# Windowed attention with block summaries, a causal gate and two projections: the order of every engine written by hand

## The chip, the cores and the metric

The kernel runs on one core of a Trainium2 chip. The core has five engines with a queue each, which the profile names PE (TensorE, matrix products; PEld is its loading of the stationary operand), DVE (VectorE), ACT (ScalarE), POOL (GpSimd) and SP (here only the issuer of DMAs). Every engine works off its own queue in order. An instruction whose inputs are not there yet waits, and all that stands behind it on that engine waits too. The metric is device time in microseconds (us); the executions measured took 295.82 us in the median of three (294.51 to 297.52).

## The reference, cut to what matters

```
B, H, S, D = 4, 8, 768, 64;  block, window = 32, 16
k_sum = max over each block of 32 keys;  v_sum = mean over each block of 32 values
scores_l = q k^T / sqrt(D)          # kept where |i - j| < 16, else -1e9
scores_s = q k_sum^T / sqrt(D) + log(32)
a = softmax([scores_l, scores_s]);  y = a @ [v, v_sum]
x = y as (B, S, 512)
gate = sigmoid(sum over 5 taps of conv_w[t] * x shifted by 4 - t rows, causal)
out = (gate * (x @ w_val)) @ w_out
```

All arrays are float32 as the reference sees them; the weights reach the kernel as 8-byte numbers, which it takes apart itself.

## The kernel before, in words

**Tiles.** A batch of 768 rows is cut into three groups of 256 rows (`SG`), so there are 12 groups, g = 0 to 11. Of a group's four pairs of heads, two make a *unit*: 24 units, u = 0 to 23, two to a group. A unit goes through these stages; the names are those that the changed code gives them, the lines those of the kernel before.

- Scores: 16 float32 matmuls (L314) into one PSUM tile `s`, of which there is only one buffer. DVE scales, masks and takes the row's minimum with one custom instruction per tile, eight a unit (`sn`, `nm`, L327; *snorm* in the change). ACT takes the exponentials, eight a unit, with the row sums as a by-product (L338, *exps*).
- Norm: DVE adds 1e-9 and takes the reciprocal (`ri`, L347, L348), POOL multiplies the probabilities by it, two instructions of 480 columns (L351).
- Transposes: four on PE into one PSUM tile `pt` with a single buffer (L364, *tp*), and a copy of it by ACT into `pts` (L365, *pcopy*), twice a unit.
- x: attention times values, 16 matmuls (L381; group 0 has 16 more, L383) into one PSUM tile `x`. ACT copies it out (*xout*): rounded as `xh` (L391) and whole as `xf` (L392), and POOL takes the difference `xl` (L394).
- Gate: for groups 0 to 4 ACT writes the last tap into PSUM tile `g` (L404, *ginit*); in later groups DVE does (L408). DVE adds the four other taps, eight instructions a unit (L412, *taps*). They read `xf` and four halo columns before it, which POOL fills when a group begins (L291, L293). ACT takes tanh (L416, *gate*).

Per group come the projections. *val* (L446, `proj_val`) is two tiles, each of 24 matmuls that build a float32 product from the halves `xh`, `xl` and the two halves of `wv`; group 0 uses plain float32 (L431). A val tile is evicted by DVE, which multiplies it by the gate (`gf`, L450), by ACT, which rounds (`gh`, L451), and by POOL, which takes the rest (`gl`, L452). *out* (L464, `proj_out`) is two tiles of 12 matmuls each over `gh`, `gl` and the halves of `wo`; ACT evicts it (`ob`, L470) and SP stores it. PSUM holds three tiles `pp` for projections.

**Side work.** For each later batch, four pieces of keys are reduced by DVE (`prep_k`, L123, L133), four pieces of values by a tree of additions on POOL (`prep_v`, L144). PE transposes the four sums (`prep_vs`, L179), ACT copies them, and DMAs spread them into the value tile (`fill_vs`, L191). The weights are converted to float32 at the start by ACT and DVE (`to_f32`, L204 to L211) and split into halves by ACT and POOL (`split_w`, L246, L247).

**What sets the order.** A loop over steps s (L541) emits, for each step, side work, the norm of unit s - 1, projections, x and gate of unit s - 2, scores of unit s, projections, and the transposes of unit s - 1. Of this text only SP keeps the order, and in the first two steps PE within a step; the others are ordered by the framework's scheduler, from its own estimate of times. Projections are issued from a budget (`PROJ_RATE`, `VAL_COST`, `OUT_COST`, L483). Side work has due steps in tables (L46 to L50).

Of the kernel before, what the change touches and what calls it, by code (L numbers as in the profile page):

```python
# [41 lines left out]
LAG_N, LAG_T, LAG_AV = 1, 1, 2  # L42
PROJ_RATE = 2.03
VAL_COST, OUT_COST = 2.64, 2.6
ACT_TAP_G = 5
LOADS = "k0 q0 m k1 q1 n0 i k2 q2 n1 k3 q3 n2 n3 v0 c w0 w1 w2 w3 Q"  # L46
CONVERT = {"wv": (0, 0, 1, 0), "wo": (3, 4, 3, 5)}
SPLIT = {"wv": (6, 2, 5, 2), "wo": (6, 5, 6, 6)}
LOAD_K = ((2, 3, 4, 4), (0, 1, 2, 3))
PREP_K = ((3, 4, 5, 5), (2, 2, 4, 4))  # L50
# [3 lines left out]
def tile_attention_then_gated_conv(  # L54
# [145 lines left out]
    def to_f32(dst, raw, n, nm, bufs):  # L200
# [3 lines left out]
        nc.scalar.activation(sc, high.bitcast(F32), AF.Copy, scale=REBIAS)  # L204
        hi = sc.bitcast(U32)
# [5 lines left out]
        nc.vector.scalar_tensor_tensor(d, hi, 0x80000000, d, ALU.bitwise_and, ALU.bitwise_or)  # L211
# [37 lines left out]
    def load_cw():  # L249
        dst = cwt.rearrange("p a k -> p (a k)")  # L250
        if not wide:
            nc.sync.dma_start(dst, cw)
# [3 lines left out]
        to_f32(dst, raw, NPR * NK, "cw", 1)  # L256

    def load_w4(nm, src, ks):
        for k in ks:
            load_w(nm, src, k, wk, ("gh", "gl")[k % 2])  # L260
# [5 lines left out]
        w=lambda i: load_w4("wv", wv, (i,)),  # L266
# [31 lines left out]
    def stage_s(u):  # L298
        b, th, hp = units[u]
        g = b * NTH + th  # L300
        sp = ps_s.tile([P, 2, 512], F32, tag="s", name=f"s_{u}")
        sn = wk.tile([P, NP, KW], F32, tag="sn", name=f"sn_{u}")
        p = wk.tile([P, NP, KW], F32, tag="p", name=f"p_{u}", bufs=3)
        nm = wk.tile([P, NP], F32, tag="nm", name=f"nm_{u}", bufs=4)
        rs = wk.tile([P, NP], F32, tag="rs", name=f"rs_{u}", bufs=4)
        for r in range(2):
            pr = 2 * hp + r
            for j in range(TPU // 2):
                for e in range(2):
                    for h in range(2):  # L310
                        i = 2 * j + e
                        t = th * TPU + i
                        c = 2 * r + j
                        nc.tensor.matmul(  # L314
                            sp[64 * e : 64 * e + 64, h, c * KW : c * KW + KW],
                            qbd[g % NQB][64 * h : 64 * h + 64, pr, i * QT : i * QT + QT],
                            ktile[b, pr][64 * h : 64 * h + 64, STEP * t : STEP * t + KW],
                            start=True,
                            stop=True,
                        )  # L320
            for j in range(TPU // 2):
                for h in range(2):
                    t = th * TPU + 2 * j
                    mv = 0 if t == 0 else (2 if t == NT - 2 else 1)
                    n = TPU * r + 2 * j + h
                    c = 2 * r + j
                    nc.vector.tensor_tensor_reduce(  # L327
                        sn[:, n, :],
                        sp[:, h, c * KW : c * KW + KW],
                        mask[:, mv, :],  # L330
                        -1.0 / math.sqrt(D),
                        3.0e38,
                        ALU.add,
                        ALU.min,
                        nm[:, n : n + 1],
                    )
        for n in range(NP):
            nc.scalar.activation(  # L338
                p[:, n, :], sn[:, n, :], AF.Exp, bias=nm[:, n : n + 1], scale=-1.0,
                accum_out=rs[:, n : n + 1],  # L340
            )
# [16 lines left out]
    def stage_t(u, r):  # L358
# [3 lines left out]
        pt = ps_t.tile([P, TPU, P], F32, tag="pt", name=f"pt_{u}_{r}")  # L362
        for i in range(TPU):
            nc.tensor.transpose(pt[:KW, i, :], s["p"][:, TPU * r + i, :], ident)  # L364
        nc.scalar.copy(s["pts"][:, TPU * r : TPU * r + TPU], pt[:KW])  # L365

    def stage_av(u):
        b, th, hp = units[u]
        g = b * NTH + th
        s = st.pop(u)  # L370
        xp = ps_x.tile([P, 2, SG], F32, tag="x", name=f"x_{u}")
        v = vtile[g]
        for r in range(2):
            for i in range(TPU):
                for h in range(2):
# [16 lines left out]
        nc.scalar.copy(x[:, prs, c0 : c0 + SG], xp)  # L392
# [239 lines left out]
```

## Time and profile before

| | |
|---|---|
| executions | 295.82 us median, 294.51 to 297.52 |
| the profiled execution | 294.14 us |
| its span, first to last instruction | 292.4 us |
| mean granted clock of TensorE | 0.977 |
| instructions | 7376 |
| HBM read, written | 34.51 MB, 6.29 MB |

Times in the profile are in microseconds from the start of the span; the mean of one instruction is in ns. In a row of the timeline the first number is the start, the second the duration of the merged instructions, `x4` their count, and the bracket holds the idle time of the engine before them with what ended it. In a group's row (`L412 DVE ...`) the busy time and the mean follow the bar, then the idle time before the group and its releasers. In a table by stretches the columns are the length and then, for PE, PEld, DVE, ACT and POOL, busy time and count, then the granted clock, the DMA share and GB/s. A float32 matmul leaves two records on PE. Pieces of the chain of waits give start, length, engine and line.

### The profile page before, as it was taken

What the parts mean: (1) busy time and instruction counts of PE and PEld (TensorE: products, weight loads), DVE (VectorE), ACT (ScalarE), POOL (GpSimd) and SP (SyncE); (2) the same over time, 40 slices, a digit from 0 to 9 for tenths busy, and PEclk for the clock granted to TensorE, in tenths of its full rate; (3) what the DMA queues carried; (4) which work ended last, traced back from release to release, by engine and by line L of the source; (5) the groups of instructions that cost most, each with busy time, mean ns of one, the idle gap of its engine ahead of it and who ended that gap; (6) DMA issues with size and microseconds to landing.
All of it is one profiled execution on the core that took longest, in us unless ns stands there. A gap on an engine that the chain in (4) does not pass through costs nothing.

```text
span 292.4 us, 7376 instructions
## 1 busy us (share of the span) xinstructions
PE 248.7 (85%) x2660; PEld 201.0 (69%) x2660; DVE 209.9 (72%) x761; ACT 183.1 (63%) x593; POOL 150.2 (51%) x187
## 2 busy tenths in 40 slices
PE   1238475999998999979978889799999998999995
PEld 0126363777886777957856767597887887898893
DVE  1949799597866887782769879987976697963710
ACT  1429472686883968877387648696678667745131
POOL 1132847468675397295059566646454355270421
PEclk9999959599999999999999999999999999999999
DMA  7999940771367854701828908426054340101011
GB/s 220 402 261 313 327 182 17 214 288 56 110 152 246 234 187 121 239 8 36 231 101 194 319 18 207 189 92 154 2 151 129 103 127 23 72 2 72 2 72 72
DMA packets 15148, 43.44 MB, mean 149 GB/s; under 512 B 2512, under 2 KB 3280, under 8 KB 13936
## 3 DMA queue, kind: packets, MB, share of 16 engines
q1 hardware_dynamic: 15111, 42.98, 47.9%
q8 instruction: 21, 0.34, 0.5%
q14 instruction: 16, 0.12, 0.1%
HBM read 34.51 MB, written 6.29 MB: 140 GB/s over the span
## 4 chain that ended last, share of the span: by engine, by line
PE 40%; DMA 23%; DVE 18%; ACT 8%; POOL 4%; SPq 4%; issue 3%; ACTq 0%; POOLq 0%; DVEq 0%
PE val L446 14%; PE out L464 13%; DMA k<-in_kT_dram 8%; DMA v<-in_vw_dram 7%; DVE g L412 7%; PE x L381 4%; DMA out_dram<-ob 4%; ACT p L338 4%; PE s L314 4%; PE pt L364 3%; DMA raw_wo<-in_wo_dram 2%; DVE sn L327 2%; SPq L191 2%; DMA vT<-in_vT_dram 2%; DVE ks L123 2%
## 5 line engine op out<-in xcount | busy, mean ns | idle before, releaser
L412 DVE SCALAR_TENSOR_TENSOR g<-xf,cwt,g 128x256 f32<-128x256 f32 x192 | 93.5, 487 | 9.0 <-ACT g L404 4.7
L338 ACT ACTIVATE p<-sn,nm 128x120 f32<-128x120 f32 x192 | 73.9, 392 | 22.3 <-DVE nm L327 22.1
L446 PE MATMUL val<-xh,wv 128*128 128x256 f32 x352 | 69.0, 285 | 0.6 <-ACT ob L470 0.6
L351 POOL TENSOR_TENSOR p<-p,ri 128x480 f32<-128x480 f32 x48 | 47.4, 1007 | 29.4 <-DVE ri L348 19.8
L464 PE MATMUL out<-wo,gh 128*128 128x512 f32 x192 | 59.3, 400 | 0.5 <-DVE gf L450 0.5
L446 PEld LDWEIGHTS val<-xh,wv 128*128 128x128 f32 x352 | 55.3, 188 | 3.2 <-issue 1.1
L327 DVE CUSTOM_DVE_ANT_0 sn<-s,mask 128x120 f32<-128x120 f32 x192 | 43.4, 277 | 14.2 <-PE s L314 14.1
L446 PE MATMUL val<-xl,wv 128*128 128x256 f32 x176 | 50.6, 288 | 0.7 <-POOL xl L394 0.7
L314 PE MATMUL s<-k,qbd 64*64 64x120 f32 x768 | 37.8, 292 | 12.4 <-DVE nm L327 6.9
L394 POOL TENSOR_TENSOR xl<-xf,xh 128x512 fp32r<-128x512 f32 x22 | 28.4, 1291 | 27.6 <-ACT xf L392 27.6
L452 POOL TENSOR_TENSOR gl<-gf,gh 128x512 fp32r<-128x512 f32 x24 | 31.2, 1301 | 20.6 <-ACT gh L451 20.6
L144 POOL TENSOR_TENSOR vT<-vT 128x384 f32<-128x384 f32 (+3 forms) x48 | 27.7, 582 | 23.6 <-DMA vT<-in_vT_dram 15.9
L464 PEld LDWEIGHTS out<-wo,gh 128*128 128x128 f32 x192 | 34.6, 188 | 7.4 <-issue 0.8
L381 PE MATMUL x<-pts,v 120*64 120x64 f32 x768 | 35.7, 231 | 4.6 <-ACT pts L365 3.9
L464 PE MATMUL out<-wo,gl 128*128 128x512 f32 x96 | 36.7, 407 | 2.4 <-POOL gl L452 2.4
L381 PEld LDWEIGHTS x<-pts,v 120*64 120x64 f32 x768 | 28.7, 139 | 14.5 <-issue 5.3
L314 PEld LDWEIGHTS s<-k,qbd 64*64 64x64 f32 x768 | 23.1, 140 | 22.6 <-DVE nm L327 6.5
L364 PE MATMUL pt<-ident,p 128*120 128x128 f32 x192 | 32.2, 291 | 6.3 <-ACT pts L365 3.2
L338 ACT ACTIVATION_READ_ACCUMULATOR p<-sn,nm 128x1 f32 x192 | 37.5, 195 | 0.0
L365 ACT COPY pts<-pt 120x512 f32<-120x512 f32 x48 | 28.1, 586 | 10.9 <-PE pt L364 10.9
L446 PEld LDWEIGHTS val<-xl,wv 128*128 128x128 f32 x176 | 33.0, 188 | 2.8 <-issue 1.3
L364 PEld LDWEIGHTS pt<-ident,p 128*120 128x120 f32 x192 | 22.2, 143 | 12.5 <-POOL p L351 4.8
(52 smaller groups left out, 277.2 us busy)
## 6 DMA issues: line engine op xcount, KB each, us to landing
k<-in_kT_dram SPq DMA_DIRECT2D x16, 478.0 KB
vT<-in_vT_dram SPq DMA_DIRECT2D x16, 384.0 KB
out_dram<-ob SPq DMA_DIRECT2D x24, 256.0 KB
qbd<-in_qT_dram SPq DMA_DIRECT2D x11, 512.0 KB
v<-in_vw_dram SPq DMA_DIRECT2D x11, 512.0 KB
v<-in_vw_dram SPq DMA_DIRECT2D x22, 128.0 KB
raw_wv<-in_wv_dram SPq DMA_DIRECT2D x4, 512.0 KB
raw_wo<-in_wo_dram SPq DMA_DIRECT2D x4, 512.0 KB
```

The source lines that it names most:

```text
L314: nc.tensor.matmul(sp[64 * e : 64 * e + 64, h, c * KW : c * KW + KW], qbd[g % NQB][64 * h : 64 * h + 64, pr, i * QT : i * QT + QT], ktile[ ...
L327: nc.vector.tensor_tensor_reduce(sn[:, n, :], sp[:, h, c * KW : c * KW + KW], mask[:, mv, :], -1.0 / math.sqrt(D), 3.0e38, ALU.add, ALU.mi ...
L338: nc.scalar.activation(p[:, n, :], sn[:, n, :], AF.Exp, bias=nm[:, n : n + 1], scale=-1.0, accum_out=rs[:, n : n + 1],)
L351: nc.gpsimd.tensor_tensor(s["p"][:, w], s["p"][:, w], ri[:, w].unsqueeze(2).broadcast_to([P, TPU, KW]), ALU.mult,)
L364: nc.tensor.transpose(pt[:KW, i, :], s["p"][:, TPU * r + i, :], ident)
L365: nc.scalar.copy(s["pts"][:, TPU * r : TPU * r + TPU], pt[:KW])
L381: nc.tensor.matmul(dst, v[:, i, c0 : c0 + D], src, start=True, stop=g > 0)
L394: nc.gpsimd.tensor_tensor(G["xl"][:, prs, :], x[:, prs, c0 : c0 + SG], G["xh"][:, prs, :].bitcast(F32), ALU.subtract,)
L412: nc.vector.scalar_tensor_tensor(gt[:, r], x[:, pr, o : o + SG], cwt[:, pr, o : o + 1], gt[:, r], ALU.mult, ALU.add,)
L446: nc.tensor.matmul(pp[:, r], w[:, ci, cs], G[x][:, ci, :], start=(n == 0), stop=(n == 11))
L452: nc.gpsimd.tensor_tensor(G["gl"][:, cos, :], gf, G["gh"][:, cos, :].bitcast(F32), ALU.subtract)
L464: nc.tensor.matmul(pp, G[gx][:, ci, si * P : si * P + P], w[:, ci, :], start=(n == 0), stop=(n == 11))
```

## The change

The scheduler's freedom is taken away: one region around the whole kernel keeps the order of the program text on all engines. The text is rewritten for this. The stages are cut into single functions (the body of each is as before, except where named below), and a `step` emits them. The first four units and the conversions are laid out op by op ahead of step 4.

```diff
-LOADS = "k0 q0 m k1 q1 n0 i k2 q2 n1 k3 q3 n2 n3 v0 c w0 w1 w2 w3 Q"
-CONVERT, SPLIT, PROJ_RATE, VAL_COST, OUT_COST, LAG_*
+LOADS = "k0 q0 m k1 q1 n0 i k2 q2 n1 k3 q3 n2 n3 v0 c Q w0 w1 w2 w3 v1 o0 o1 o2 o3"
+LOAD_K = (-4, -3, -2, -1)
+PREP_K = (-2, -1, -1, 0)
+PREP_V = (-3, -2, -1, 0)
...
-        nc.scalar.activation(sc, high.bitcast(F32), AF.Copy, scale=REBIAS)
+        nc.scalar.activation(sc, high.bitcast(F32), AF.Prelu, scale=REBIAS, alpha=-(2.0**32))
-        nc.vector.tensor_scalar(d, hi, 3, None, ALU.logical_shift_left)
+        nc.vector.tensor_scalar(d, low, 29, None, ALU.logical_shift_right)
         nc.vector.scalar_tensor_tensor(
-            d, low, 29, d, ALU.logical_shift_right, ALU.bitwise_or
+            d, sc.bitcast(U32), 3, d, ALU.logical_shift_left, ALU.bitwise_or
         )
-        nc.vector.scalar_tensor_tensor(d, hi, 0x80000000, d, ALU.bitwise_and, ALU.bitwise_or)
...
+    def proj():
+        if not queue:
+            return lambda: None
+        mm, ev, g, i = queue.pop(0)
+        pp = mm(g, i)
+        return lambda: ev(g, i, pp)
...
+    def late_loads(s):
...
+                if w == PREP_K[i]:
+                    prep_k(b, i)
+                if w == PREP_V[i]:
+                    prep_v(b, i)
+            if w == 0:
+                prep_vs(b)
+                fill_vs(b * NTH)
...
+    def step(s, late=lambda: None):
+        early_loads(s)
+        norm(s - 1)
+        ev = proj()
+        mm_x(s - 2)
+        ev()
+        xout(s - 2)
+        ginit(s - 2)
+        mm_s(s, 0)
+        mm_s(s, 1)
+        snorm(s, 0)
+        snorm(s, 1)
+        tp(s - 1, 0)
+        exps(s, 0)
+        pcopy(s - 1, 0)
+        exps(s, 1)
+        taps(s - 2)
+        ev = proj()
+        tp(s - 1, 1)
+        pcopy(s - 1, 1)
+        ev()
+        gate(s - 2)
+        if units[s - 2][2] == NHP - 1 and s > 3:
+            queue_proj((s - 2) // NHP)
+        late()
+        late_loads(s)
...
+    prep_k(0, 0)
+    mm_s(0, 0)
+    snorm(0, 0)
+    exps(0, 0)
...
+    exps(2, 0)
+    split_w("wv", 1)
+    conv_w("wv", 3)
+    exps(2, 1)
+    early_loads(2)
+    mm_s(3, 0)
+    mm_s(3, 1)
+    ppv = [val_mm(0, 0)]
+    taps(0)
+    gate(0)
+    ginit(1)
+    norm(2)
+    snorm(3, 0)
+    snorm(3, 1)
...
+    val_ev(0, 1, ppv[1])
+    split_w("wv", 3)
+    conv_w("wo", 0)
+    split_w("wo", 0)
+    late_loads(3)
+
+    def late4():
+        for k in range(1, 4):
+            conv_w("wo", k)
+            split_w("wo", k)
+        queue.extend((out_mm, out_ev, 0, si) for si in range(SG // P))
+
+    step(4, late4)
+    for s in range(5, NU + 2):
+        step(s)
+    while queue:
+        proj()()
...
-    ... tc.manual_schedule(engines={_mybir.EngineType.SP}):
+    ... tc.manual_schedule():
```

(The guards `if s < NU` and the like, which leave out stages at both ends, are cut from `step`.) Further:

- The queue of projections holds both val tiles, then both out tiles of a group. Each `proj()` takes one item from its head, emits its matmuls and gives back a function that emits its eviction; between the two stand x, or the second half of the transposes.
- Within a val tile the eight matmuls per row half that read `xh` come first and the four that read `xl` last; within an out tile the eight that read `gh` first, the four that read `gl` last. Group 0's val uses one PSUM tile for both row halves and one eviction for both.
- The key and value pieces of batch b are loaded in steps 6b - 4 to 6b - 1 and prepared in steps 6b - 3 to 6b, at the end of a step. `wo` and the second value tile are loaded with the first loads, `wo` in the buffers of `xh` and `xl`; the first loads of q for group 1 stand ahead of `wv`.
- The conversion of the convolution's weights is taken out of their load and stands after unit 1's norm.

More of the change, by code (lines that the diff above doesn't have):

```diff
@@ L249, in load_cw @@
     def load_cw():
[L250 removed]
         if not wide:
[L252 removed]
+            nc.sync.dma_start(cwt.rearrange("p a k -> p (a k)"), cw)
             return
@@ L296, in group, with mm_s @@
         return grp[g]
-    def stage_s(u):
+    def mm_s(u, r):
         b, th, hp = units[u]
         g = b * NTH + th
[L301 to L321, printed above, removed]
@@ L474, in tile_attention_then_gated_conv @@
     queue = []
-    issued = set()
-    def can_issue(item):
-        f, g, i = item
-        if f is proj_val:
-            return len(ready["wv" if g else "wvf"]) == 4
-        return (g, NHP - 1) in issued and len(ready["wo"]) == 4
-    def run_proj(budget):
-        while budget > 0:
-            item = next((it for it in queue if can_issue(it)), None)
-            if item is None:
-                break
-            queue.remove(item)
-            f, g, i = item
-            f(g, i)
-            if f is proj_val:
-                issued.add((g, i))
-            budget -= VAL_COST if f is proj_val else OUT_COST
-        return min(budget, PROJ_RATE)
@@ new lines, in late_loads @@
+    def late_loads(s):
+        g, hp = divmod(s, NHP)
+        for b in range(1, B):
+            w = s - b * NTH * NHP
+            for i in range(NPR):
+                if w == PREP_K[i]:
[5 more added lines that the diff above has]
+                fill_vs(b * NTH)
+        if hp == NHP - 1 and 1 <= g < NG - 1:
+            load_v(g + 1)
+            if (g + 1) % NTH:
+                fill_vs(g + 1)
@@ new lines, in tile_attention_then_gated_conv @@
+    prep_k(0, 0)
+    mm_s(0, 0)
+    snorm(0, 0)
+    exps(0, 0)
+    prep_k(0, 1)
+    mm_s(0, 1)
+    prep_v0(0)
+    snorm(0, 1)
+    exps(0, 1)
+    prep_k(0, 2)
+    mm_s(1, 0)
+    prep_v0(1)
+    snorm(1, 0)
+    norm(0)
+    exps(1, 0)
+    prep_k(0, 3)
+    tp(0, 0)
+    mm_s(1, 1)
+    pcopy(0, 0)
+    prep_v0(2)
+    snorm(1, 1)
+    tp(0, 1)
+    prep_v0(3)
+    exps(1, 1)
+    pcopy(0, 1)
+    place_vs0()
+    fill_vs(1)
+    norm(1)
+    conv_cw()
+    tp(1, 0)
+    pcopy(1, 0)
+    mm_x(0)
@@ new lines, in tile_attention_then_gated_conv @@
+    tp(1, 1)
+    pcopy(1, 1)
+    xout(0)
+    ginit(0)
+    conv_w("wv", 0)
+    mm_s(2, 0)
+    mm_s(2, 1)
+    snorm(2, 0)
+    snorm(2, 1)
+    mm_x(1)
+    xout(1)
+    conv_w("wv", 1)
+    split_w("wv", 0)
+    conv_w("wv", 2)
+    exps(2, 0)
[12 more added lines that the diff above has]
+    snorm(3, 1)
+    exps(3, 0)
+    tp(2, 0)
@@ new lines, in tile_attention_then_gated_conv @@
+    pcopy(2, 0)
+    val_ev(0, 0, ppv[0])
+    exps(3, 1)
+    split_w("wv", 2)
+    ppv.append(val_mm(0, 1))
+    taps(1)
+    gate(1)
+    tp(2, 1)
+    pcopy(2, 1)
+    early_loads(3)
+    norm(3)
+    val_ev(0, 1, ppv[1])
[9 more added lines that the diff above has]
+    step(4, late4)
```

287 lines of the change are left out of this document (139 added, 148 removed).

## The prediction, made before the changed kernel was run

> **What bounds the kernel now.** I read the page's busy shares and its clock row first, then the pace of the units (the reciprocal of the softmax sums, one per unit, is a good clock), then single stretches of the timeline.
>
> ```profile
> PE 248.7 (85%) x2660; PEld 201.0 (69%) x2660; DVE 209.9 (72%) x761; ACT 183.1 (63%) x593; POOL 150.2 (51%) x187
> ...
> PEclk9999959599999999999999999999999999999999
> ```
>
> ```profile
> 71.12 0.20 DVE L348 RECIPROCAL ri<-ri 128x8 f32<-128x8 f32 x1
> 256.39 0.20 DVE L348 RECIPROCAL ri<-ri 128x8 f32<-128x8 f32 x1
> ```
>
> ```profile
> 172.40:191.70 19.30, 16.26 (x192) 12.46 (x191) 18.44 (x75) 14.24 (x50) 12.39 (x18) 1.00 0.51 153
> 227.00:246.40 19.40, 18.57 (x234) 15.19 (x230) 14.84 (x61) 13.40 (x47) 9.12 (x9) 1.00 0.32 95
> ```
>
> Unit 4 is normalised at 71.1 us, unit 23 at 256.4: 185.3 / 19 = 9.75 us a unit, 19.5 a pair. A head of 71 us stands before, 36.0 us of mostly projections behind. No engine bounds the whole: in 172.4:191.7 DVE is busy 18.44 of 19.3 us, in 227:246.4 PE 18.57 of 19.4. The free order hands the time from one to the other. So the question for an order by hand is which waits it fixes into every step.
>
> **One pair of steps in the new order.** Durations on PE and at its borders:
>
> ```profile
> L314 PE MATMUL s<-k,qbd 64*64 64x120 f32 x768 | 37.8, 292 | 12.4 <-DVE nm L327 6.9 <-DVE k L133 5.4
> ```
>
> ```profile
> 110.92 1.15 PE L381 MATMUL x<-pts,v 120*64 120x64 f32 x32
> 210.38 0.64 PE L314 MATMUL s<-k,qbd 64*64 64x120 f32 x16
> 211.09 0.28 DVE L327 CUSTOM_DVE_ANT_0 sn<-s,mask 128x120 f32<-128x120 f32 x1 [0.42 <-PE s L314]
> 83.14 0.60 PE L364 MATMUL pt<-ident,p 128*120 128x128 f32 x4
> 83.50 1.17 PE L464 MATMUL out<-wo,gh 128*128 128x512 f32 x4
> 280.49 2.83 PE val L446 x24
> 283.32 5.49 PE out L464 x24
> ```
>
> 768 score records over 24 units are 32 a unit, so the 16 of one row are half of it: with 0.57 to the next work (210.38 to 210.95), scores cost 1.14, and DVE starts 0.71 after the first of them. x costs 1.15, four transposes 0.36 (83.14 to 83.50), val 2.83, an out tile 5.49 / 2 = 2.75, 0.229 a matmul.
>
> ```profile
> 211.90 0.08 DVE L327 DVE_READ_ACCUMULATOR2_ANT nm<- 128x1 f32 x1
> 262.17 0.49 DVE L408 TENSOR_SCALAR g<-xf,cwt 128x256 f32<-128x256 f32 x1
> 262.69 2.06 DVE L412 SCALAR_TENSOR_TENSOR g<-xf,cwt,g 128x256 f32<-128x256 f32 x4
> 255.59 0.68 DVE L450 SCALAR_TENSOR_TENSOR gf<-gt,val 128x512 f32<-128x512 f32 x1
> 256.30 0.62 ACT L451 CAST gh<-gf 128x512 fp32r<-128x512 f32 x1
> 201.98 0.62 ACT L451 CAST gh<-gf 128x512 fp32r<-128x512 f32 x1
> 202.68 1.30 POOL L452 TENSOR_TENSOR gl<-gf,gh 128x512 fp32r<-128x512 f32 x1 [1.41 <-ACT gh L451]
> 256.19 0.16 DVE L347 TENSOR_SCALAR ri<-rs 128x8 f32<-128x8 f32 x1
> 256.74 1.94 POOL L351 TENSOR_TENSOR p<-p,ri 128x480 f32<-128x480 f32 x2 [6.67 <-DVE ri L348]
> ```
>
> Four sn take 0.81 (211.09 to 211.90): 1.6 a unit. Taps: 0.52 each, so 2 x 2.08 = 4.16 a unit while ACT writes the first tap (groups 0 to 4), 2 x 2.60 = 5.2 plus a little, say 5.24, later. gf to gh 0.71, gh to PE 0.68 (0.62 and a semaphore), gh to gl 0.70, gl 1.30. Norm 0.4, multiplies of 0.97.
>
> Counting the queue: a group adds four items (two val, two out), each step takes two, so val of group g runs in step 2g+4 and out in 2g+5, each alternating. In a val step the second gf stands on DVE **behind all taps**, and the first out tile stands at the head of PE's next step, ahead of x and scores. That tile's first four matmuls need only the first half of gh; the fifth waits. Behind it on PE queue x, scores, transposes and the second out tile, and DVE waits for the scores. So a pair is a loop through both engines:
> - DVE: sn 1.6 + taps 5.24 = 6.84, then gf to gh 0.71, gh to PE 0.68;
> - PE: 8 matmuls 1.83, x 1.15, scores 1.14, transposes 0.36, out 2.75, transposes 0.36, val 2.83, x 1.15, then 0.71 to DVE: 12.28.
> Sum 20.5 us a pair, 19.4 with the shorter taps. (The other way round the odd step on DVE needs 6.84 + norm 0.4 + gf 0.6, which is 0.7 shorter than PE's share and hidden.) PE idles in each such pair from its fourth out matmul on: DVE's 0.71 + 6.84 + 0.71 + 0.68 = 8.9 against PE's own 1.14 + 0.36 + 2.83 + 0.36 + 0.92 = 5.6, some 3.4 us. The gl of that tile comes 0.70 + 1.30 after gh, just when its eight matmuls are through: covered.
>
> **Batch preparation** now stands in that order too:
>
> ```profile
> L144 POOL TENSOR_TENSOR vT<-vT 128x384 f32<-128x384 f32 (+3 forms) x48 | 27.7, 582 | 23.6 <-DMA vT<-in_vT_dram 15.9 <-DVE nm L327 6.6
> L144 POOL TENSOR_TENSOR vsT<-vT 128x24 f32<-128x24 f32 x12 | 2.8, 231 | 0.7
> L123 DVE TENSOR_REDUCE ks<-k 128x24 f32<-128x768 f32 x16 | 15.2, 950 | 14.6 <-DMA k<-in_kT_dram 14.6
> L133 DVE COPY k<-ks 128x84 f32<-128x84 f32 (+1 forms) x32 | 9.7, 342 | 0.2
> ```
>
> prep_v is (27.7 + 2.8) / 12 = 2.54 us on POOL, prep_k (15.2 + 9.7) / 16 = 1.56 on DVE. In steps 6, 12 and 18 the last prep_v follows gl, and prep_vs puts transposes of it on PE **ahead of the out tile**: PE waits 2.54 longer, then runs the tile whole (2.75) where only 0.46 was left: 5.0 with the transposes' 0.2. Three times: 15 us. Two prep_k behind the taps of steps 5, 11 and 17 push norm by 3.1; 0.7 to 1.9 of it is covered by PE. Then POOL's multiplies push gl and, behind gl, the halo copy for which the taps wait: together about 3 each, lower bound 1.2. Loads move by some steps; each is issued one or two steps (10 to 20 us) ahead of its use, and out stores wait in SP's queue behind nothing longer: zero, and a late transfer would be seen at prep_k.
>
> **Head.** The order by op gains where the old one mixed conversions: one DVE op (0.69 us alone) less for each of eight weight blocks, units 0 and 1 packed closely. But it then strings conversions on ACT between the exponentials, and the last of them come late:
>
> ```profile
> L204 ACT ACTIVATE sc_wo<-raw_wo 128x512 f32<-128x512 f32 x4 | 2.7, 671 | 2.6 <-DMA raw_wo<-in_wo_dram 1.6 <-ACT sc_wo L204 0.9
> 36.77 0.69 DVE L211 SCALAR_TENSOR_TENSOR wst<-sc_wo,wst 128x512 uint32<-128x512 uint32 x1
> 0.73 1.28 ACT L338 ACT_TABLE_LOAD   x1 [0.73 <-PEq L618]
> 27.81 0.66 ACT L204 ACTIVATE sc_wv<-raw_wv 128x512 f32<-128x512 f32 x1
> ```
>
> The last wv block can be converted no earlier than before (27.8, its transfer now behind 0.5 MB of q: 29.5) and by ACT's queue not before about 35 (unit 1's xout at 29.5 by the same count, then three conversions of 0.67, two casts as long as a gh, four exponentials, 0.69 on DVE). From 35: taps of unit 0 4.2, norm and sn 2, gf 0.6, taps 4.2, norm, gf, gh: 48. POOL then has multiplies 1.9, gl, two weight splits of 1.3 and prep_v ahead of the halo: 55.5. Taps 4.2 and gate: 60. Three wo blocks in a row, each 0.67 + 0.69 + 0.62 on ACT and DVE: 66, last split 67.5, end of the out tile, x, 0.71: scores of unit 5 reach DVE at 70.5, of unit 6 at 81 (out, transposes, val, x and 0.71 are 8.6, and 2.6 for the two prep_k). Bounds: 75, if the transfer alone sets 29.5; 91, if the new Prelu needs a table load of 1.28 on each of some eight changes to and from Exp. The trace has one load for Exp, Copy and Tanh and no Prelu; I take none.
>
> **Tail.** From the last norm: rest of two steps, then two val and two out tiles with nothing beside: out waits for gf (after the taps of unit 23), ends 27.8 after norm, and the old end (ob at 288.88, span 292.4) adds 3.5: 31.5 against 36.0 now.
>
> **Clock.** PE's longer waits have a second price:
>
> ```profile
> 34.00:38.00 4.00, 0.00 (x0) 0.00 (x0) 2.77 (x4) 3.28 (x12) 1.72 (x2) 0.88 1.02 407
> 38.00:44.00 6.00, 5.92 (x16) 4.71 (x16) 5.96 (x16) 4.66 (x15) 3.12 (x3) 0.51 0.31 125
> 46.00:51.00 5.00, 2.26 (x58) 1.82 (x53) 4.96 (x12) 1.72 (x3) 3.21 (x5) 0.97 0.01 3
> 51.00:57.00 6.00, 5.79 (x15) 4.48 (x16) 3.68 (x15) 3.83 (x13) 2.43 (x4) 0.50 0.80 187
> 38.09 5.49 PE L431 MATMUL val<-xf,wvf 128*128 128x256 f32 x12 [4.15 <-ACT xf L392]
> 58.74 1.89 PE L431 MATMUL val<-xf,wvf 128*128 128x256 f32 x8
> 147.80 0.65 PE L364 MATMUL pt<-ident,p 128*120 128x128 f32 x4 [2.14 <-ACT pts L365]
> 288.88 0.60 ACT ob L470
> ```
>
> After a wait of 4.15 the granted clock is 0.51 and twelve matmuls take 5.49, against 1.89 x 12/8 = 2.83 at full clock: 2.66 lost. After 2.14 (at 147.8) nothing. The three waits at prep_vs are over 7 us: nearest to the first row, 3 x 2.66 = 8.0 (bounds 0 and 8.0). The 3.4 us waits lie between the rows; I take 0, upper bound five of them, 13.3. The Trainium skill ("TensorE: Matmul & The Clock Gate", section "Part 1") halves the clock after an idle window of about 3.4 us that runs free. By that rule the 3.4 us waits almost never fill a window, which speaks for 0. But the stretch 46:51, PE busy 2.26 of 5 us and no wait over 2.2, was followed by 0.50 as well, so the row says the rule may be too kind.
>
> **Sum.** From unit 6 at 81: five pairs of 20.5 and three of 19.4 are 160.7 to unit 22; to unit 23 and its norm 6.84 + 0.71 + 0.68 + 1.83 + 1.15 + 0.71 + 6.84 = 18.8; prep_vs 15, prep_k 2 x 3 = 6: norm at 281.5. Tail 31.5: 313. Clock 8: span 321. The profiled run took 294.14 at span 292.4, so 1.7 more: about **322 us**, against 294.14. The median of the runs, 295.82, lies 1.7 above that run; I don't add it.
>
> **Rivals.**
> - No lasting clock loss: the same loop, clock 1.00 behind the waits: 322 - 8 = 314. For it: the rows at 147.8; against: 38:44.
> - The clock also halves at the 3.4 us waits: 322 + 13 = 335. For it: 46:51.
> - Shorter preparation: prep_vs's operands are ready early (POOL idle 49%) and the head ends at 75: 322 - 15 - 8 - 6 = 293, within 1% of now. Against it: prep_v stands behind gl in POOL's order.
> - Faster: the new order does not hold on DVE and ACT, and gf is still moved ahead of the taps. Place: gf of the second val; price: PE's 3.4 us a pair vanish and a pair takes PE's own 2 x (2.83 + 2.75 + 1.15 + 1.14 + 0.72) = 17.2, with preparation 18.8. From unit 6 to the last norm are 8.9 pairs: 81 + 8.9 x 18.8 = 248, tail 29, 1.7: 279; at the old pace of 19.5, 285. It decides if gf ends before PE has done its first four out matmuls, 3.4 us sooner than I place it.
>
> **Chances.** Forecast 0.40, no clock loss 0.24, clock at all waits 0.08, Prelu loads (333) 0.04, shorter preparation 0.08, faster 0.16. A measurement here tells about 1% (3 us) from no change. Faster by over 1% 0.18 (with a part of the shorter preparation), within 1% 0.06, slower 0.76. The range from 291 to 336 leaves out the fast case and the worst clocks; the forecast's own is 308 to 330.
>
> **What would show it.** Right: waits of PE on gh of 3 us before the fifth matmul of every first out tile; sn waiting on PE in every step; pairs of 19 to 21 us; PE waiting on POOL's vsT three times with clock 0.5 behind it; unit 4 normalised near 67. Wrong: pairs under 19, gf ahead of taps on DVE, a head under 60, or PE waits under 1 us.

## The result and the profile after

The changed kernel takes 338.16 us in the median of four runs (336.31 to 339.29). The kernel before took 296.57 beside it (294.51 to 297.52). The ratio is 1.1407, with a 95% interval of 1.1318 to 1.1495. The ratios, here and below, leave out some executions of the kernel before that were slower as a whole (298 to 301 us). The profiled execution took 336.31 us at a span of 334.5. The forecast was 322, its range 291 to 336: the direction was right, and the time lies above the range.

The page of the changed kernel, busy shares and granted clock:

```profile
PE 243.8 (73%) x2660; PEld 203.0 (61%) x2660; DVE 218.5 (65%) x750; ACT 183.7 (55%) x593; POOL 149.2 (45%) x187
...
PEclk9999796569969999999689899799699899799698
```

Every engine does about the work that it did before, in a span 42.1 us longer. PE's share falls from 85 to 73%, and the clock row now has dips to 6 and 7 from the middle to the end, where the row of before showed only 9 from its second quarter on.

The units' clock, the reciprocal of the softmax sums, for units 4 and 23:

```profile
71.04 0.20 DVE L350 RECIPROCAL ri<-ri 128x8 f32<-128x8 f32 x1
300.08 0.20 DVE L350 RECIPROCAL ri<-ri 128x8 f32<-128x8 f32 x1
```

Unit 4 is where it was (71.12 before). From there to unit 23 it takes 229.0 us instead of 185.3: 43.8 more. The rest, 34.4, is 1.6 shorter. So the whole loss lies in the steps.

What the engines wait for there, in the view of waits (us in total, times, the longest):

```profile
DVE sn L327 <- PE s L310: 65.8, 20, 8.5
ACT gh L467 <- DVE gf L466: 38.4, 22, 3.1
PE vsp L175 <- POOL vsT L140: 23.3, 3, 8.2
PE out L480 <- ACT gh L467: 22.6, 8, 3.5
```

DVE waits for scores in 20 steps, PE for the rounded gate product eight times and for the values' sums three times. All of these waits were in the forecast. One of them, in a late pair, in the timeline:

```profile
188.09 0.68 DVE L466 SCALAR_TENSOR_TENSOR gf<-gt,val 128x512 f32<-128x512 f32 x1
188.80 0.62 ACT L467 CAST gh<-gf 128x512 fp32r<-128x512 f32 x1 [2.96 <-DVE gf L466]
189.47 2.07 PE L480 MATMUL out<-wo,gh 128*128 128x512 f32 x4 [3.48 <-ACT gh L467]
191.35 1.80 PE L480 MATMUL out<-wo,gl 128*128 128x512 f32 x4
193.08 1.15 PE L386 MATMUL x<-pts,v 120*64 120x64 f32 x32
194.16 1.05 PE L310 MATMUL s<-k,qbd 64*64 64x120 f32 x32
195.28 0.28 DVE L327 CUSTOM_DVE_ANT_0 sn<-s,mask 128x120 f32<-128x120 f32 x1 [6.19 <-PE s L310]
```

This is the loop through both engines: the product `gf` behind the taps, `gh` behind it, the second half of the out tile on PE, x, scores, and only then DVE again, after 6.19 us of waiting. Two things in it can be measured against the forecast. PE's wait is 3.48 us (3.4 forecast). But the eight matmuls behind it, from 189.47 to 193.08, take 3.6 us where 1.83 were reckoned. In an early pair, behind a wait of 2.32 us, the way from the first of the eight to the scores is 3.15 us (119.49 to 122.64) and here 4.69 (189.47 to 194.16), 1.5 more:

```profile
119.49 1.20 PE L480 MATMUL out<-wo,gh 128*128 128x512 f32 x4 [2.32 <-ACT gh L467]
122.64 1.05 PE L310 MATMUL s<-k,qbd 64*64 64x120 f32 x32
```

The table by stretches says why (the granted clock is the number behind the five busy times and counts):

```profile
119.50:121.60 2.10, 2.10 (x10) 1.41 (x10) 0.00 (x0) 0.43 (x1) 2.09 (x2) 1.00 0.92 337
189.40:191.30 1.90, 1.83 (x4) 1.49 (x5) 0.00 (x0) 0.52 (x2) 1.80 (x2) 0.52 0.81 325
...
214.00:215.00 1.00, 1.00 (x5) 0.35 (x3) 0.82 (x3) 0.00 (x0) 0.92 (x2) 0.50 0.07 16
289.00:290.20 1.20, 1.20 (x5) 0.45 (x4) 0.00 (x0) 0.00 (x0) 1.20 (x2) 0.50 0.00 0
```

Behind waits of 3.48 us, in the last three rows (they end at 189.47, 212.20 and 287.36), the clock is halved; behind the wait of 2.32 us, in the first row, it is not.

### The profile page after: what moved, and what is told of

It reads as the page before. It is cut to its first block, busy times and chain, and to the rows that moved or that the text cites. A ratio compares the mean times of both kernels' runs of the same rounds, so it can differ in the third digit from the quotient of the medians.

```text
span 334.5 us, 7354 instructions
## 1 busy us (share of the span) xinstructions
PE 243.8 (73%) x2660; PEld 203.0 (61%) x2660; DVE 218.5 (65%) x750; ACT 183.7 (55%) x593; POOL 149.2 (45%) x187
## 3 DMA queue, kind: packets, MB, share of 16 engines
q1 hardware_dynamic: 15102, 43.17, 42.1%
## 4 chain that ended last, share of the span: by engine, by line
PE 40%; DVE 28%; POOL 8%; issue 3%; ACT 3%; POOLq 0%; DVEq 0%; ACTq 0%
PE out L480 18%; DVE g L431 17%; PE val L456 8%; PE x L386 6%; PE s L310 5%; DVE sn L327 4%; POOL gl L468 3%; POOL vT L140 3%; PE pt L366 2%; DVE g L427 2%; ACT gh L467 2%; DVE gf L466 2%; POOL p L353 2%; DVE wst L203 1%; DVE ks L119 1%
## 5 line engine op out<-in xcount | busy, mean ns | idle before, releaser
L480 PE MATMUL out<-wo,gh 128*128 128x512 f32 x192 | 63.7, 468 | 31.2 <-ACT gh L467 22.6
L327 DVE CUSTOM_DVE_ANT_0 sn<-s,mask 128x120 f32<-128x120 f32 x192 | 40.9, 278 | 65.9 <-PE s L310 65.8
L480 PEld LDWEIGHTS out<-wo,gh 128*128 128x128 f32 x192 | 39.4, 220 | 44.9 <-ACT gh L467 26.1
L456 PE MATMUL val<-xh,wv 128*128 128x256 f32 x352 | 50.4, 285 | 0.0
L456 PEld LDWEIGHTS val<-xh,wv 128*128 128x128 f32 x352 | 44.6, 189 | 0.1
L487 ACT ACTIVATE ob<-out 128x512 f32<-128x512 f32 x24 | 14.3, 596 | 39.9 <-PE out L480 18.9
L467 ACT CAST gh<-gf 128x512 fp32r<-128x512 f32 x24 | 14.9, 619 | 38.4 <-DVE gf L466 38.4
L310 PE MATMUL s<-k,qbd 64*64 64x120 f32 x768 | 27.5, 281 | 10.8 <-DVE k L129 9.9
L386 PE MATMUL x<-pts,v 120*64 120x64 f32 x768 | 32.5, 239 | 2.1 <-ACT pts L370 1.1
L480 PE MATMUL out<-wo,gl 128*128 128x512 f32 x96 | 31.0, 452 | 0.0
L140 POOL TENSOR_TENSOR vT<-vT 128x384 f32<-128x384 f32 (+3 forms) x48 | 27.1, 565 | 2.8
```

The source lines that it names most:

```text
L140: nc.gpsimd.tensor_tensor(dst, src[:, :, :n], src[:, :, n : 2 * n], ALU.add)
L310: nc.tensor.matmul(st[u]["sp"][64 * e : 64 * e + 64, h, c * KW : c * KW + KW], qbd[g % NQB][64 * h : 64 * h + 64, pr, i * QT : i * QT + QT ...
L327: nc.vector.tensor_tensor_reduce(s["sn"][:, n, :], s["sp"][:, h, c * KW : c * KW + KW], mask[:, mv, :], -1.0 / math.sqrt(D), 3.0e38, ALU.a ...
L386: nc.tensor.matmul(dst, v[:, i, c0 : c0 + D], src, start=True, stop=g > 0)
L456: nc.tensor.matmul(pp[:, r], w, x, start=(n == 0), stop=(n == len(terms) - 1))
L480: nc.tensor.matmul(pp, x, w, start=(n == 0), stop=(n == len(terms) - 1))
```

## The experiments

Times are medians; ratios are against the kernel before, measured beside each run (medians 296.29, 297.29 or 295.75 us). The theory: (A) the loss is the order itself, in three parts, the late eviction in the pair's loop, the transposes that wait for the last preparation of values, and the slow clock that both waits leave behind. Rivals: (B) in each run another cause or a bound that remains, and (C) that the new operations and loads cost the time.

### The order given back, and given to one engine

The changed text, with the order by hand on SP alone:

```diff
-schedule_with_timeline_sim=True) as tc, tc.manual_schedule():
+schedule_with_timeline_sim=True) as tc, tc.manual_schedule(engines={_mybir.EngineType.SP}):
```

> The text of the changed kernel, with its operations, tables and loads, but the order by hand taken off all engines except SP: PE, DVE, ACT and POOL are ordered by the framework's scheduler again. Theory A (the order is the loss, not the operations): the fixed waits vanish, 285 to 305 us. Rival C (the changed operations, Prelu, the new order of terms or the late loads cost the time): 320 us or more.

289.15 us, ratio 0.977 (0.9705 to 0.9834). C falls: the new operations, loads and places of side work gain 7 us when the scheduler orders them; the order costs 338.16 - 289.15 = 49. In this run unit 4 is normalised at 63.16 and unit 23 at 257.35: the head is 8 us shorter than before, the tail (288.1 - 257.35 = 30.7) 5.3, the steps are 9 longer.

The same with `{SP, DVE}`:

> The text of the changed kernel, with the hand-written order binding on VectorE (and SyncE's queue, as in all of these) alone; the scheduler orders TensorE, ScalarE and GpSimd. Theory A: a pair is a loop that needs both the late second eviction on VectorE and the out tile at the head of TensorE's step. With VectorE's order alone TensorE can put x, scores and transposes ahead of that tile, and most of the loss goes: 295 to 308 us. Rival B: VectorE's late eviction alone costs the time: 325 or more.

323.76 us, ratio 1.0962 (1.0895 to 1.1029): far from A's time, just under B's 325. And with `{SP, PE}`:

> The text of the changed kernel, with the hand-written order binding on TensorE (and SyncE's queue) alone; the scheduler orders VectorE, ScalarE and GpSimd. Theory A: VectorE takes the second eviction ahead of or between the taps, as in the kernel with the taps split, and GpSimd the preparation of the values' sums sooner: 287 to 303 us. Rival B: the out tile at the head of TensorE's step and the transposes ahead of it decide by themselves: 320 or more.

316.82 us, ratio 1.0729 (1.0657 to 1.0801): neither. Each order alone, with the rest fitted round it, keeps (323.76 - 289.15) / 49.0 = 71% and 56% of the loss, so the loss as a whole does not need both engines' order. But the two losses lie in different places. The norms of unit 4:

```profile
81.52 0.20 DVE L350 RECIPROCAL ri<-ri 128x8 f32<-128x8 f32 x1
```

```profile
61.44 0.20 DVE L350 RECIPROCAL ri<-ri 128x8 f32<-128x8 f32 x1
```

Against the run with SP alone (63.16), DVE's order loses 18.4 us in the head, and 13.3 in the steps from unit 4 to unit 23 (normalised at 289.02; 207.5 against 194.2). PE's order loses nothing in the head and 33.0 in the steps (unit 23 at 288.60; 227.2). Both orders together lose 7.9 in the head and 34.9 in the steps. So for DVE's order theory A was right about the steps, which keep 38% of their loss, and had not thought of the head; for PE's order it falls. The waits in the steps are others than with both. With DVE's order, PE's new wait is in front of val; with PE's order, PE waits for `gl`, which POOL makes behind a piece of value preparation that waits for its load (a row of the first, then three of the second kernel):

```profile
260.88 2.08 PE L456 MATMUL val<-xh,wv 128*128 128x256 f32 x8 [2.53 <-DVE gf L466]
```

```profile
211.82 1.00 POOL L140 TENSOR_TENSOR vT<-vT 128x384 f32<-128x384 f32 x1 [8.10 <-DMA vT<-in_vT_dram]
212.78 1.26 POOL L468 TENSOR_TENSOR gl<-gf,gh 128x512 fp32r<-128x512 f32 x1
214.10 1.22 PE L480 MATMUL out<-wo,gl 128*128 128x512 f32 x2 [4.27 <-POOL gl L468]
```

In the first, the late evictions of DVE hold back the next group's val instead of the out tile. In the second, the scheduler put a preparation ahead of `gl` whose data SP's order brought later. How much of each remaining loss such waits make was not separated.

### The late eviction

The taps are split in their two halves, with the second eviction between them:

```diff
-            taps(s - 2)
+            taps(s - 2, (0,))
         ev = proj()
...
         ev()
         if s - 2 < NU:
+            taps(s - 2, (1,))
             gate(s - 2)
```

> The changed kernel with one thing moved: the second eviction of a step (gf, gh, gl of the second val tile, or ob) stands between the two halves of the taps instead of behind both. Theory A (the loop gf behind all taps, gh, out tile at the head of PE, x, scores, DVE): gf comes 2.6 us earlier in groups 5 to 11 (2.1 in the earlier ones), PE's wait of 3.48 shrinks to about 0.9 and no longer halves the clock, pairs of late groups go from 22.7 to about 18.3, of early ones from 20.0 to 18; in all some 30 us less: 303 to 312. Rival B (the pairs are long because in-order engines lose time everywhere, not at this one place): another wait takes its place, the time stays over 325.

306.85 us, ratio 1.0379 (1.0312 to 1.0445): 31.3 us less, as A says. The wait at the out tile is now

```profile
264.21 1.21 PE L480 MATMUL out<-wo,gh 128*128 128x512 f32 x4 [0.86 <-ACT gh L467]
```

with the four matmuls behind it at full clock (1.21 instead of 2.07), and a late pair takes 18.58 instead of 22.73.

The same place from PE's side: x and scores moved ahead of the first out tile of a step, DVE's order untouched.

```diff
-        ev = proj()
+        ev = None if xfirst else proj()
         mm_x(s - 2)
-        ev()
+        if not xfirst:
+            ev()
...
         snorm(s, 1)
+        if xfirst:
+            ev = proj()
         tp(s - 1, 0)
...
         pcopy(s - 1, 0)
+        if xfirst:
+            ev()
```

> The changed kernel with the loop cut at its other end: where an out tile would stand at the head of a step, x and the scores go ahead of it on PE (its eviction on ACT goes behind the first copy of the transposes); DVE's order is untouched, gf stays behind all taps. Theory A (a loop through gf, out, x and scores): DVE gets its scores some 4 us sooner in each pair, late pairs go from 22.7 to about 18.7, PE's wait from 3.5 to about 1.1 with the clock at 1.00; 305 to 315 in all. Rival B (only the late gf counts, whatever stands behind it): 330 or more.

320.85 us, ratio 1.0825 (1.0669 to 1.098): between A and B. The mechanism works, the wait at the out tile is 0.85 to 0.94 and a late pair 19.4 (unit 20 normalised at 262.99, unit 22 at 282.38). But A had counted on more: the three waits for the values' sums stay (6.99, 8.13, 8.16), and unit 4 is normalised 2.1 later. Of the eight pairs from unit 6 to unit 22 only the two late ones without preparation gain 3.3 each, all eight together 7.1; 6.0 more come between unit 22 and the last norm and 2.4 in the tail, and the head up to unit 6 takes 2.7 back.

### The values' sums

One number changed, the last preparation one step earlier:

```diff
-PREP_V = (-3, -2, -1, 0)
+PREP_V = (-3, -2, -1, -1)
```

> The changed kernel with one number changed: the last preparation of the values' sums one step earlier, so that GpSimd has it ready before the transposes on TensorE. Theory A (the forecast's term): three waits of 7.0 to 8.2 us on TensorE become ordinary waits of 2.3 to 3.5 us at the out tile, 13 us less, and 2 to 5 us less of slow clock behind them: 320 us (316 to 326). Rival B: TensorE would have waited for the eviction anyway, or GpSimd's later multiplies and splits give it back: 331 or more.

323.06 us, ratio 1.0941 (1.0881 to 1.1002): 15.1 less, inside A's 316 to 326. The three waits of 7.0 to 8.2 become waits at the out tile of 1.84, 3.04 and 3.01.

The other way to take the wait from PE's path: the transposes moved behind the first transposes of p of the next step.

```diff
-            if w == 0:
-                prep_vs(b)
-                fill_vs(b * NTH)
...
             pcopy(s - 1, 0)
+        if s < NU and s > 6 and s % (NTH * NHP) == 1:
+            prep_vs(s // 6)
+            fill_vs(s // 6 * NTH)
```

> The changed kernel with the value-sum transposes (with the copy and the DMAs behind them) moved from the end of steps 6, 12, 18, where PE waits for POOL's last addition tree, into the next step behind the copy of the first transposes. Theory A: the three waits of 7.0 to 8.2 us shrink to the usual 2.3 to 3.5, each pair with them loses 5 us of wait and about 1.5 of halved clock: 3 x 6.5 = 19 less, about 319. Rival B (the sums then reach the value tile late and x waits for the DMAs instead): under 8 us less, 330 or more.

327.55 us, ratio 1.1075 (1.0994 to 1.1156): 10.6 less, a half of what A said. The new price is at x, which now waits 1.1 to 1.2 us for the sums' DMA, three times; and where PE had waited for the sums, it now waits for `gh`, with the clock halved behind it in two of the three places (one of them the second row):

```profile
107.47 1.03 PE L386 MATMUL x<-pts,v 120*64 120x64 f32 x28 [1.21 <-DMA v<-vs]
...
232.40 2.01 PE L480 MATMUL out<-wo,gh 128*128 128x512 f32 x4 [3.43 <-ACT gh L467]
```

### The clock

Throwaway matmuls fill PE's waits: 12 ahead of the first out tile of groups 5, 6, 8 and 9, and 30 ahead of the transposes of the sums. They write a tile that is overwritten. (The condition in the code, `g % NTH != 1`, leaves out group 10 as well as group 7, so that the last of the five waits which the expectation names is not filled: it stays at 3.46 us, with the clock at half behind it.)

```diff
+    def warm(pp, n):
+        w = wsplit["wo"][:, 0, 0]
+        for _ in range(n):
+            nc.tensor.matmul(pp, w[:, :P], w, start=True, stop=True)
...
+            warm(pp, 12)
...
+        warm(ps, 30)
```

> The changed kernel with throwaway matmuls in PE's fixed waits and nothing moved: 12 (2.75 us) ahead of the first out tile of groups 5, 6, 8, 9 and 10, where PE waits 3.48 us for gh, and 30 (6.9 us) ahead of the three sets of value-sum transposes, where it waits 7.0 to 8.2 us; what they write is overwritten by the real tile. Theory A (the waits cost twice, once as waits and once as a clock halved behind them): granted clock 1.00 behind these waits, the eight matmuls after a wait take 1.9 us in place of 2.8 to 3.7 and x 1.1 in place of 1.1 to 1.9, pairs of the late groups 20.9 us in place of 22.7; in all 5 x 1.8 + 3 x 1.5 = 13.5 us less, about 325 us against 338. Rival B (the low clock in the late groups comes with something else than idle time, such as load or heat, or costs nothing because DVE is the bound): clock stays near 0.90, time 336 to 341.

327.72 us, ratio 1.1073 (1.0998 to 1.1148): 10.4 less by doing more work; A's 325 was near, and B falls: the mean clock rises from 0.901 to 0.953. With 12 of them a late pair takes 21.2 instead of 22.7 (norms of units 19 and 21: 248.94, 270.15), so the loop at full clock is 21.2, and the slow clock behind one wait costs 1.5. The rows show a filled wait:

```profile
254.31 3.02 PE L175 MATMUL out<-wo 128*128 128x512 f32 x12
258.94 1.20 PE L488 MATMUL out<-wo,gh 128*128 128x512 f32 x4 [0.68 <-ACT gh L473]
259.98 1.10 PE L488 MATMUL out<-wo,gl 128*128 128x512 f32 x4
```

How long a wait is enough? The last kernel of this part leaves the whole computation out: 64 bursts of 27 to 36 matmuls with 512 columns, and between them DVE chains that let PE wait 1.5 to 5.4 us.

> Leaves out the whole computation: 64 bursts of 27 to 36 matmuls of 512 columns (6 to 8 us at full clock), between them a chain of one to eight DVE instructions and a copy by ACT for which the next burst waits, so that PE idles 1.5 to 5.5 us. Theory A1 (a halved clock comes from the share of idle time in some window of about 3.4 us, so that 2.3 us sometimes do it and 3.5 us nearly always): first matmuls at half speed after none of the waits under 2 us, some of those of 2.2 to 3.2, all above 3.5. Theory A2 (a window must be wholly idle): none below 3.4, and only those near 6.8 always.

806.18 us. A matmul at full clock takes 0.237 us here (30 in 7.11). I call a burst slowed when it takes over 1 us longer than that; the slowed ones lose 1.3 to 2.9 us.

| wait ahead of the burst, us | bursts | slowed |
|---|---|---|
| 1.49 to 1.67 | 7 | 0 |
| 2.02 to 3.07 | 21 | 9 |
| 3.24 to 3.60 | 8 | 6 |
| 3.76 to 5.41 | 28 | 28 |

Theory A2 falls; A1 holds but for one burst, which kept its clock after 3.60.

Waits of one length are found with and without the loss. The second number is the time of the burst, the last its count of matmuls; 30 and 33 take 7.1 and 7.8 us at full clock:

```profile
33.77 7.11 PE L92 MATMUL pp<-z,w 128*128 128x512 f32 x30 [2.02 <-ACT z L100]
223.86 9.37 PE L92 MATMUL pp<-z,w 128*128 128x512 f32 x33 [2.02 <-ACT z L100]
291.10 7.77 PE L92 MATMUL pp<-z,w 128*128 128x512 f32 x33 [3.60 <-ACT z L100]
302.63 9.39 PE L92 MATMUL pp<-z,w 128*128 128x512 f32 x33 [3.76 <-ACT z L100]
```

So there is no threshold in the wait's length alone. What decides can be read from the granted clock of this run: all its changes lie on one grid with a step of 3.413 us, whatever the bursts do. The first two bursts above follow waits of the same 2.02 us. The table by stretches, cut at that grid, holds each wait and what comes behind it (first the length and PE's busy time; the granted clock is the third number from the end):

```profile
29.84:33.25 3.41, 1.91 (x9) 1.25 (x7) 1.31 (x3) 0.00 (x0) 0.00 (x0) 1.00 0.00 0
33.25:36.66 3.41, 2.89 (x13) 2.38 (x14) 0.00 (x0) 0.37 (x1) 0.00 (x0) 1.00 0.00 0
220.98:224.40 3.42, 1.40 (x6) 0.86 (x5) 1.30 (x3) 0.37 (x1) 0.00 (x0) 1.00 0.00 0
224.40:227.81 3.41, 3.41 (x9) 2.64 (x8) 0.00 (x0) 0.00 (x0) 0.00 (x0) 0.50 0.02 5
```

The first wait is split by the grid into 1.50 and 0.52 us of idle time, and the clock stays. The second lies in one stretch, with 2.02 us idle, and the next stretch runs at half clock from end to end. All stretches of the run from its tenth microsecond on go by this: at full clock, the 123 with at most 1.85 us idle were followed by full clock and the 43 with at least 1.96 by half; at half clock, the 42 with at most 0.57 idle were followed by full clock and the 23 with at least 0.65 by half again. So what counts is how much of a wait falls into one stretch of the grid. A wait of 2 us can fall into one or be split; a wait of more than twice 1.9 leaves at least 1.9 in one of two neighbours, wherever it falls, and from 3.76 us on all bursts were slowed.

### Together

Split taps and the earlier preparation, the two edits above in one kernel:

> The kernel with the second eviction between the two halves of the taps, and one number more: the last value sum of a batch is prepared one step earlier, at the end of steps 5, 11, 17, where POOL has time, so that its transposes find it ready. Theory A (each of PE's waits for vsT, still 5.6 us there, costs itself and some 1.5 us of halved clock): 3 x 7 = 21 us less than 306.9, about 286. Rival B (the wait turns up at the out tile behind it, which needs gh and gl of the same step anyway): gain under 8 us, 299 or more.

286.97 us, ratio 0.9701 (0.9605 to 0.9797), as expected: faster than before, and 51.2 us less than the changed kernel. Apart, the two edits gave 31.3 and 15.1. With x first as well:

> All three repairs together: eviction between the halves of the taps, last value sum a step earlier, x and scores ahead of the first out tile. Theory A: no fixed wait is left, a pair costs PE's own 17.2 us or little more (17.5), nine pairs at 1 us less than with the first two alone: about 277, below both kernels. Rival B (a new wait, of the transposes for POOL's multiplies or of ACT's order, takes their place): 285 or more.

288.83 us, ratio 0.9763 (0.9666 to 0.986): B. A late pair does shrink (240.36 to 258.15, 17.8 against 18.6), but unit 4 comes 2.1 later (73.17), and the scores, now ahead of the out tile, run into the last preparation of keys, which stands behind DVE's taps:

```profile
153.18 0.64 PE L310 MATMUL s<-k,qbd 64*64 64x120 f32 x16 [2.75 <-DVE k L129]
```

From unit 4 to unit 23 it takes 185.0 us, as without x first (185.1). Last, split taps and earlier preparation with the head left to the scheduler, the order by hand beginning at step 5:

```diff
+    with tc.manual_schedule():
-    for s in range(5, NU + 2):
-        step(s)
-    while queue:
-        proj()()
+        for s in range(5, NU + 2):
+            step(s)
+        while queue:
+            proj()()
```

> The kernel with split taps and earlier preparation of the values' sums, with the order by hand beginning at step 5; all ahead of it (the head with the weight conversions) is ordered by the scheduler. Theory A: unit 4 is normalised near 63 us instead of 71, as where the scheduler orders all, and the rest stays: 279 us (276 to 282). Rival B: the gain of the head is lost where the two orders meet, or the later steps wait for weights that come no sooner: 285 or more.

278.05 us, ratio 0.9414 (0.9369 to 0.9458): A. The page, and the units' clock:

```profile
PE 235.4 (86%) x2660; PEld 197.5 (72%) x2660; DVE 205.7 (75%) x750; ACT 183.1 (67%) x593; POOL 149.4 (54%) x187
```

```profile
60.45 0.20 DVE L350 RECIPROCAL ri<-ri 128x8 f32<-128x8 f32 x1
245.88 0.20 DVE L350 RECIPROCAL ri<-ri 128x8 f32<-128x8 f32 x1
```

The steps take 185.4 us, the same as before the change (185.3) and 8.8 less than with the changed text ordered by the scheduler (194.2). What this best version gains is the head, 60.45 instead of 71.12, and the tail, 275.1 - 245.88 = 29.2 instead of 36.0: together 17.5 of a span that is 17.3 shorter.

## Why the prediction failed, point by point

**Right: the order by hand costs, by the loop that was named.** The forecast's waits are all there: out tile 3.48 us (3.4), in early pairs 2.32, the values' sums three times, scores in every step. The steps can be compared pair by pair, from the first `sn` of an even unit to that of the next. Four of these `sn`:

```profile
84.02 0.27 DVE L327 CUSTOM_DVE_ANT_0 sn<-s,mask 128x120 f32<-128x120 f32 x1
...
181.28 0.28 DVE L327 CUSTOM_DVE_ANT_0 sn<-s,mask 128x120 f32<-128x120 f32 x1 [1.06 <-PE s L310]
...
204.01 0.28 DVE L327 CUSTOM_DVE_ANT_0 sn<-s,mask 128x120 f32<-128x120 f32 x1 [1.04 <-PE s L310]
...
279.17 0.28 DVE L327 CUSTOM_DVE_ANT_0 sn<-s,mask 128x120 f32<-128x120 f32 x1 [1.06 <-PE s L310]
```

| units | 6-8 | 8-10 | 10-12 | 12-14 | 14-16 | 16-18 | 18-20 | 20-22 | sum |
|---|---|---|---|---|---|---|---|---|---|
| forecast, with its clock term | 27.1 | 19.4 | 22.4 | 28.2 | 20.5 | 23.5 | 28.2 | 20.5 | 189.8 |
| measured | 28.4 | 20.1 | 21.0 | 27.8 | 22.7 | 24.0 | 28.4 | 22.7 | 195.2 |

Six of eight pairs lie within 1.4 us. The two that don't, 14-16 and 20-22, are the late pairs without preparation, and each is 2.2 too long. Of these, 1.5 are the clock (22.73 against 21.2 with the waits filled). The other 0.7 are the loop itself, and early pair 8-10, where the clock stays full, shows them too (20.1 for 19.4): from the first score record to DVE it takes 1.12 us (194.16 to 195.28 above) and not the 0.71 read from the kernel before, for DVE now starts behind all 32 records; out and val tiles took 0.1 to 0.2 more each. In pair 16-18 the same wait and slow clock stand (the row 214:215 above), but the sum hides them: pair 10-12, with the keys and without the slow clock, took 1.4 less than forecast, so the two pieces of keys cost less than the 3 reckoned.

**Wrong: "The 3.4 us waits lie between the rows; I take 0".** This is the step that failed: a term of the sum put at 0 that measured 1.5 us a wait. Behind these waits the clock stands at 0.50 to 0.52 in the table by stretches, and the way through out tile and x to the scores took 4.69 instead of the 3.15 of an early pair. The five waits fall in pairs 14-16, 16-18 and 20-22, between unit 22 and unit 23's norm (20.9 against 18.8 forecast) and in the tail (34.4 against 31.5), where the last of them stands:

```profile
309.81 2.07 PE L480 MATMUL out<-wo,gh 128*128 128x512 f32 x4 [3.48 <-ACT gh L467]
311.69 1.91 PE L480 MATMUL out<-wo,gl 128*128 128x512 f32 x4
```

Five times 1.5 are 7.5 of the 13.5 us by which the span (334.5) lies above the forecast's 321, the largest single part; the tail's share is argued from these rows, not taken apart. The rival "The clock also halves at the 3.4 us waits" said 335 and was given 0.08. It had the right mechanism, but its price of 2.66 a wait was too high, and that it came so near to the profiled run's 336.31 is in part luck: it had no share for the longer loop and the later head. Filling four of the five waits (and the three for the values' sums) shortened the four stretches of steps that hold them by 1.5 each (22.73 to 21.21, 23.99 to 22.49, 22.73 to 21.19, 20.91 to 19.40), although the wait's end was still set by `gh`: the clock, not only the wait, was the cost. The Trainium skill ("TensorE: Matmul & The Clock Gate", section "Part 1: The HAM clock gate (the "warmup" mystery)") puts the return to half clock after at least one idle window of about 3.4 us. By it, I gave the rival too small a chance. The bursts were slowed after 2.02 us once in five and after 3.76 always, and stretches that were idle for 1.96 of 3.41 us were enough. So the measurement decides against a wholly idle window, and agrees with the window's length and with its running free. The row 46:51 of the kernel before had spoken for a loss too, and I had seen it and set it aside.

**Right in kind, near in size: preparation of values.** Three times 5.0 and 2.66 of clock were forecast, 23 in all. Taking the wait away alone gave 15.1, because a wait for `gh` of 1.8 to 3.0 us and a slow clock take its place; with the late eviction mended too it gave 306.85 - 286.97 = 19.9. That the slow clock follows these long waits was forecast; it is in the pairs above.

**Head: 3 us too short.** Unit 4 was to be normalised near 67 and was at 71.04; scores of unit 6 were put at 81 and came at 84.02. The gate came as forecast, at 60, and what follows it was short: the last of the three weight splits ended at 69.9 (68.63 and 1.27) and not at 67.5. Each conversion was reckoned at one DVE operation of 0.69 us. But the changed text has two for each block, a shift (L202) and the joining of the halves (L203); the shift, 0.42 alone, was left out, and both took about two to four times as long while POOL was at work on two tensors of that size:

```profile
60.28 0.42 DVE L202 TENSOR_SCALAR wst<-raw_wo 128x512 uint32<-128x512 uint32 x1
61.63 1.77 POOL L404 TENSOR_TENSOR xl<-xf,xh 128x512 fp32r<-128x512 f32 x1 [5.46 <-ACT sc_wo L200]
62.19 1.50 DVE L202 TENSOR_SCALAR wst<-raw_wo 128x512 uint32<-128x512 uint32 x1
63.37 1.44 POOL L241 TENSOR_TENSOR wo<-wst,wo 128x512 fp32r<-128x512 f32 x1
63.79 1.56 DVE L203 SCALAR_TENSOR_TENSOR wst<-sc_wo,wst 128x512 uint32<-128x512 uint32 x1
...
70.55 1.91 PE L480 MATMUL out<-wo,gl 128*128 128x512 f32 x4
```

The out matmuls that follow them then run at half clock (1.91 for four), where I reckoned full. How much of the 3 us is due to which was not separated. That the scheduler's head is faster by 8 to 11 us is shown by two runs, and by a third that PE's order by hand does not lose this gain (61.44), while DVE's does (81.52). I had named a gain there ("units 0 and 1 packed closely") and not that the order by hand could lose it again.

**The other rivals.** No lasting clock loss (314): falls with the same rows. Prelu's table loads (333): the trace shows one load of 1.28, as before. Shorter preparation (293): PE did wait 7.0 to 8.2 us for POOL; one number in the text made it come true, and the pair's loop was still there at 323. Faster (279): not in the changed kernel, whose order held on all engines; with the eviction moved between the taps a late pair took 18.6, where I had reckoned 17.2 for an eviction wholly out of the way.

**Sums that don't add up in the forecast.** 8.9 less 5.6 is 3.3 (3.4 was written), the tail's 27.8 and 3.5 are 31.3 (31.5), and out, transposes, val, x and 0.71 are 7.8 (8.6 was written; 70.5, 7.8 and 2.6 give the 81 that was used). None of them moves the forecast by over 0.2 us.

**Sum.** Steps from unit 6 to 22: 5.5 too low; unit 22 to the last norm 2.1, tail 2.9, head 3.0: 13.5 in all. The range ended where the rival ended, at 336, and left nothing for a head that comes later as well.

## What to carry to other kernels

Where an order is written by hand, go round every loop that crosses two engines and ask what stands in front of the instruction that the other engine waits for; here eight to ten tap operations ahead of one eviction cost 31 us, and splitting them in two gave that back. Price a wait of TensorE not by its length alone: in this kernel each 3.5 us wait cost another 1.5 us of half clock, and waits from 2 us on must carry a part of that price. And order by hand only what pays: the free order of the head was worth 9 us (286.97 to 278.05), while the mended steps only equalled those of the kernel before (185.4 us and 185.3), if they were 8.8 shorter than the scheduler's order of the same text.

## What the runs showed of the hardware

- The clock's fall needs no idle stretch of 3.4 us: 9 of 21 bursts were slowed after waits of 2.02 to 3.07 us, and none of 7 after 1.49 to 1.67, all of 28 from 3.76 on (one of these the first burst of the run).
- In the run of bursts the granted clock changes only on a grid of 3.413 us. A stretch of it with at least 1.96 us idle was followed by half clock, one with at most 1.85 us idle was not; half clock ended after a stretch with at most 0.57 us idle. In the kernels the changes lie on a grid of the same step; the limits are less sharp there (half clock after 1.61 us idle at the least, full clock kept after 1.95 at the most).
- The fall can come after the wait. In the kernel with only the preparation moved, the four matmuls after a wait of 3.48 us took 1.21 in one pair, and 2.07 in another; and 2.07 once after a wait of only 2.32:

```profile
133.84 2.07 PE L480 MATMUL out<-wo,gh 128*128 128x512 f32 x4 [2.32 <-ACT gh L467]
...
180.27 1.21 PE L480 MATMUL out<-wo,gh 128*128 128x512 f32 x4 [3.48 <-ACT gh L467]
181.32 1.86 PE L480 MATMUL out<-wo,gl 128*128 128x512 f32 x4
```

  In the pair at 180.27 the four matmuls behind those took 1.86: the clock fell about a microsecond after PE had resumed.
- In the changed kernel's head, DVE's joining operation on two SBUF tensors of 128x512 words took 0.69 us alone and 1.28 to 1.70 beside a POOL operation on two such tensors; its shift on one tensor took 0.42 alone and up to 1.50 so. It then ended a fixed time behind POOL's operation: 0.29 us for the shift (63.69 behind 63.40 above), 0.54 to 0.55 for the joining (65.35 behind 64.81).
